# Attention output with probabilities as the stationary operand, V plus a column of ones as the moving one, scaled with tokens on partitions, transposed by DMA

## The chip, the cores and the metric

The kernel runs on one core of a Trainium2 chip. The metric is device time in microseconds (us) of one execution, of the slowest core; here there is only one. A kernel is run several times, and its time is the median. A profile comes from one execution, so its span can lie anywhere in the spread of the timed runs.

Engines in the profile are PE (TensorE matmuls), PEld (TensorE weight loads), DVE (VectorE), ACT (ScalarE), POOL (GpSimd) and SP (SyncE, which issues most DMAs here). A matmul has a stationary operand (`lhsT`, which a weight load puts into the array) and a moving operand (`rhs`, which streams through it). PSUM is the memory that matmuls write to, divided into banks; SBUF is the one from which they read. To evict a PSUM tile is to copy it out, so that its bank can be used again. A semaphore, a DMA or a bank that an instruction needs can make it wait; where the text says that A waits for B, the profile inferred it. "L1064" is line 1064 of the kernel whose profile is shown.

## The reference, cut to what matters

```python
def _A_ref(x, k_cache, v_cache, wq, wo):     # x: (1, 2048, 1024), 32 query heads, 4 kv heads, Dh = 128
    W = min(4096, max(256, Sk // 4))         # 512 keys per head
    q = (x @ wq) ...                         # heads apart
    k, v = last W rows of the caches, repeated 8 times
    scores = einsum('bhqd,bhkd->bhqk', q, k) * Dh ** (-0.5)
    p = softmax(scores)
    o = einsum('bhqk,bhkd->bhqd', p, v)
    return o (heads side by side) @ wo

mod = silu(c) @ w_mod                        # six vectors: sa, ca, ga, sb, cb, gb
h = layernorm(x) * (1 + ca) + sa
x = x + ga * _A_ref(h, ...)
h = layernorm(x) * (1 + cb) + sb
x = x + gb * ((silu(h @ w_gate) * (h @ w_up)) @ w_down)
```

All inputs are bfloat16. (`...` marks what is cut or told in words.)

## The kernel before

The attention part runs 128 steps: 4 chunks of 512 tokens times 32 heads. One step is, on PE: 4 matmuls of scores (`s_ps`), 8 of a later head's query projection (`q_ps`), 8 of an earlier group's output projection (`a_ps`), and 4 that multiply probabilities with V (`o_ps`). Each has 512 moving columns. Scores are kept with keys on partitions, so a softmax row sum is a sum over partitions. The kernel before makes it in three parts: VectorE adds the four key blocks (`psA`, `psB`), once in four steps four matmuls with a block of ones add over partitions (`l_ps`, each using 32 columns of the array), and the reciprocals travel through DRAM to be broadcast to all partitions (`rb`), where VectorE multiplies them into `oT`.

```python
# ... pools: blkC has 10 buffers of 4 KB per partition, PSUM tag "mm" has 4 banks
def emit_s(g):
    # ... s_ps matmuls; pT = exp(scale * s_ps) on ScalarE
    a = wk.tile([P, 2, TCW], BF16, name="psA", tag="psA", bufs=2)
    nc.vector.tensor_tensor(out=a, in0=p[:, 0:2, :], in1=p[:, 2:4, :], op=ALU.add)
    b = wk.tile([P, TCW], BF16, name="psB", tag="psB", bufs=5)
    nc.vector.tensor_tensor(out=b, in0=a[:, 0, :], in1=a[:, 1, :], op=ALU.add)
    rec[g] = b

def emit_l(g):                                   # every fourth step
    l_ps = mm("l_ps")
    for i in range(4):
        nc.tensor.matmul(l_ps[32 * i:32 * i + 32, :], lhsT=ones_bf[:, 0:32],
                         rhs=rec.pop(g - 3 + i), start=True, stop=True)
    r = wk.tile([P, TCW], FP32, name="rinv", tag="f32", bufs=2)
    nc.scalar.activation(out=r, in_=l_ps, func=ACT.Ln)
    nc.scalar.activation(out=r, in_=r, func=ACT.Exp, scale=-1.0)
    # ... DMA to DRAM; load_rb broadcasts it back; emit_norm: oT = oT * rb on VectorE

def emit_o(g):
    # ... a new oT tile every four heads
    o_ps = mm("o_ps")
    for j in range(WT):                          # 4 key blocks
        nc.tensor.matmul(o_ps, lhsT=v_sb[:, kv, j, :], rhs=pT[g][:, j, :],
                         start=(j == 0), stop=(j == WT - 1))
    nc.scalar.copy(out=oT[(cc, hg)][:, hi, :], in_=o_ps)

def emit_wo(cc, q, u):                           # 8 matmuls; q = 0 opens a sum:
    # ...
    nc.vector.tensor_copy(out=acc[(cc, t)][:, dsl], in_=a_ps)

def load_cols(n, k, dst, add_one):               # a modulation vector, turned to columns
    # ... fetch(out=dst, in_=src)                # a small DMA
    if add_one:
        nc.vector.tensor_scalar(out=dst, in0=dst, scalar1=1.0, scalar2=None, op0=ALU.add)

# the loop of steps
for k in range(NU + 1):
    # ... emit_s(k), emit_q(k + LEAD), then the tasks planned for step k (emit_wo among them)
    if k >= 1:
        if k % 4 == 0:
            emit_l(k - 1)
        emit_o(k - 1)
# ... then the feed-forward part: gu_ps (gate and up) and d_ps (down) matmuls
```

## Time and profile before

Three runs give a median of 1292.92 us (1292.06 to 1293.39).

| | before |
|---|---|
| span of the profiled execution | 1290.1 us |
| PE busy | 1271.4 us, 99% |
| VectorE / ScalarE busy | 653.1 us, 51% / 433.7 us, 34% |
| moved by DMA | 221.08 MB |
| start to start of 512-column matmuls | 0.216 us |
| four steps, start to start | 21.16 us |

The first fence is from the page of the profile of the kernel before: span, busy time by engine (microseconds, share of the span, instructions), and the chain of work that ended last (followed back from the last instruction, at each step to what released it), as shares of the span by engine and by line.

```profile
span 1290.1 us, 15319 instructions
...
PE 1271.4 (99%) x6073; PEld 577.4 (45%) x6193; DVE 653.1 (51%) x1159; ACT 433.7 (34%) x625; POOL 1.2 (0%) x7
...
PE 95%; SPq 2%; DMA 1%; DVE 1%; issue 1%; DVEq 0%
PE gu_ps L1168 29%; PE a_ps L1095 17%; PE q_ps L1018 17%; PE d_ps L1188 15%; PE o_ps L1079 9%; PE s_ps L1031 8%; SPq L664 1%; PE l_ps L1048 1%; SPq L703 1%; DMA hT<-xn 0%; DMA wq<-in_A_wq_dram 0%; DMA wu<-in_B_w_up_dram 0%; PE row_ps L777 0
```

PE is the engine that decides: 95% of the chain is PE. What VectorE and ScalarE do costs nothing as long as no matmul waits for it. Busy PE time is of little use for a closer reading, because the ends of matmuls are modelled and overlap small gaps. Starts are better.

The next view is the groups of instructions of the kernel before: line, engine, operation, output and inputs, shapes, count | busy us and mean ns of one | idle time of the engine before them and what ended most of it.

```profile
L1079 PE MATMUL o_ps<-pT,v_sb 128*128 128x512 bf16 x510 | 131.5, 380 | 0.2
...
L1038 DVE TENSOR_TENSOR psA<-pT 128x1024 bf16<-128x1024 bf16 x128 | 87.8, 686 | 89.0 <-ACT pT L1033 88.9
...
L1069 DVE TENSOR_TENSOR oT<-oT,rb 128x1024 bf16<-128x1024 bf16 x64 | 75.4, 1218 | 1.5 <-DMA rb<-r_d 1.5
L1081 ACT CAST oT<-o_ps 128x512 bf16<-128x512 f32 x128 | 74.5, 582 | 166.4 <-PE o_ps L1079 166.4
...
L1040 DVE TENSOR_TENSOR psB<-psA 128x512 bf16<-128x512 bf16 x128 | 53.4, 417 | 0.6
...
L1048 PE MATMUL l_ps<-psB,ones_bf 128*32 128x512 bf16 x128 | 12.8, 389 | 0.3
...
L1188 PE MATMUL d_ps<-wd,guT 128*128 128x128 bf16 x56 | 3.3, 219 | 0.0
```

The mean of 380 ns for a 512-column matmul is the time from its start to its modelled end, not the time PE needs for one: the next starts 216 ns later. The three VectorE groups are 217 us of work that the change takes away, and that PE never waits for. The `l_ps` group is 12.8 us busy, but what it costs has to be read from the timeline.

This is the timeline of PE in the kernel before, in one steady part: start in us, duration, engine, line, operation, count.

```profile
344.49 1.03 PE L1079 MATMUL o_ps<-pT,v_sb 128*128 128x512 bf16 x4
345.35 1.03 PE L1031 MATMUL s_ps<-qT,kT 128*128 128x512 bf16 x4
346.21 1.89 PE L1018 MATMUL q_ps<-hT,wq 128*128 128x512 bf16 x8
347.94 1.89 PE L1095 MATMUL a_ps<-wo,oT 128*128 128x512 bf16 x8
349.76 0.40 PE L1048 MATMUL l_ps<-psB,ones_bf 128*32 128x512 bf16 x4
350.09 1.04 PE L1079 MATMUL o_ps<-pT,v_sb 128*128 128x512 bf16 x4
350.97 1.03 PE L1031 MATMUL s_ps<-qT,kT 128*128 128x512 bf16 x4
```

Read differences of starts. A plain `o_ps` group is 344.49 to 345.35, 0.86 us for four matmuls, and a group of eight 1.73 us (346.21 to 347.94). The `a_ps` group that starts at 347.94 should thus be over at 349.67, but `l_ps` starts at 349.76 (0.09 lost); it lasts 0.33 until `o_ps` starts, and that `o_ps` takes 0.88 instead of 0.86. So one `l_ps` group costs 0.09 + 0.33 + 0.02 = 0.44 us. Starts of single matmuls say the same: 0.309 us from the last `a_ps` matmul to the first `l_ps` one, 3 ns between the four, 0.322 us to the first of `o_ps`. The four run beside each other in 32-column tiles. Of the 0.44 us, 0.22 is what one 512-column matmul takes anyway, and the other 0.22 is lost on entering and leaving.

For the new cost the trace of before holds one sample, the last `d_ps` matmuls of the program, which have 128 columns and a new weight load each. They start 55.8 ns apart. The last line of the view above agrees: 3.3 us, less the 0.219 of the last one, over 55 spacings is 56 ns. How VectorE evicts tiles of such widths shows in the timeline of VectorE at the end of the kernel before (in brackets: idle time before it, and what ended that).

```profile
1281.81 0.42 DVE L1192 TENSOR_TENSOR f_10710<-d_ps,gb_bc 128x256 f32<-128x256 f32 x1 [1.64 <-PE d_ps L1188]
...
1283.38 0.29 DVE L1192 TENSOR_TENSOR f_10744<-d_ps,gb_bc 128x128 f32<-128x128 f32 x1 [0.68 <-PE d_ps L1188]
```

An eviction of 256 columns took 0.42 us and one of 128 columns 0.29 us.

### The profile page before, as it was taken

The page shows a single profiled execution, that of the slowest core. Times are in us where ns is not written, and L with a number is a line of the kernel's source. Part 1 is how long each engine was busy: PE and PEld are TensorE (multiplying, and loading weights), DVE is VectorE, ACT ScalarE, POOL GpSimd, SP SyncE. Part 2 cuts the span into 40 slices and gives each one's busy share as a digit, 9 for nine tenths or more (in the row PEclk, how much of TensorE's full clock was granted, in tenths as well). Part 3 has the DMA queues.
Part 4 walks back from the last instruction along what each step waited for, and adds up shares of the span by engine and source line. Part 5 has one row for each costly group of instructions (what it writes and reads, how often), then busy time and mean ns, then how long its engine had stood idle before and what let it go on. Part 6 is the DMA issues. An engine that isn't in the chain of part 4 may idle for free.

```text
span 1290.1 us, 15319 instructions
## 1 busy us (share of the span) xinstructions
PE 1271.4 (99%) x6073; PEld 577.4 (45%) x6193; DVE 653.1 (51%) x1159; ACT 433.7 (34%) x625; POOL 1.2 (0%) x7
## 2 busy tenths in 40 slices
PE   8999999999999999999999999999999999999998
PEld 4444444444444444444444444444444444444444
DVE  5575668976688867597865641222122111222122
ACT  4755545554555555555552111011100111011100
POOL 0000000000000000000000000000000000000000
PEclk9999999999999999999999999999999999999999
DMA  9788565567365655455657485454536445454402
GB/s 290 242 277 256 178 196 139 170 174 219 103 193 144 189 146 175 146 165 143 185 194 238 127 240 182 136 192 131 171 105 220 157 148 178 135 192 131 147 18 84
DMA packets 219939, 221.08 MB, mean 171 GB/s; under 512 B 45385, under 2 KB 205129, under 8 KB 219858
## 3 DMA queue, kind: packets, MB, share of 16 engines
q1 hardware_dynamic: 214690, 215.54, 54.5%
q10 hardware_dynamic: 5168, 4.46, 1.0%
q8 instruction: 50, 0.82, 0.3%
q14 instruction: 31, 0.25, 0.1%
HBM read 207.63 MB, written 4.47 MB: 164 GB/s over the span
## 4 chain that ended last, share of the span: by engine, by line
PE 95%; SPq 2%; DMA 1%; DVE 1%; issue 1%; DVEq 0%
PE gu_ps L1168 29%; PE a_ps L1095 17%; PE q_ps L1018 17%; PE d_ps L1188 15%; PE o_ps L1079 9%; PE s_ps L1031 8%; SPq L664 1%; PE l_ps L1048 1%; SPq L703 1%; DMA hT<-xn 0%; DMA wq<-in_A_wq_dram 0%; DMA wu<-in_B_w_up_dram 0%; PE row_ps L777 0%; DVE guT L1174 0%; DVE xn L833 0%
## 5 line engine op out<-in xcount | busy, mean ns | idle before, releaser
L1033 ACT ACTIVATE pT<-s_ps 128x1024 bf16<-128x1024 f32 x256 | 252.0, 1026 | 72.8 <-PE s_ps L1031 67.3
L1095 PE MATMUL a_ps<-wo,oT 128*128 128x512 bf16 x972 | 238.9, 379 | 2.6
L1018 PE MATMUL q_ps<-hT,wq 128*128 128x512 bf16 x994 | 236.1, 379 | 0.8 <-DVE modT L753 0.3
L1173 ACT ACTIVATE sg<-gu_ps 128x512 bf16<-128x512 f32 x112 | 66.9, 597 | 486.0 <-PE gu_ps L1168 420.4
L1174 DVE TENSOR_TENSOR guT<-gu_ps,sg 128x512 bf16<-128x512 f32 x112 | 77.4, 691 | 280.0 <-ACT sg L1173 280.0
L1168 PE MATMUL gu_ps<-hT,wu 128*128 128x512 bf16 x878 | 210.1, 379 | 2.6 <-DMA wu<-in_B_w_up_dram 1.7
L1168 PE MATMUL gu_ps<-hT,wg 128*128 128x512 bf16 x877 | 210.0, 379 | 1.1
L1188 PE MATMUL d_ps<-wd,guT 128*128 128x512 bf16 (+2 forms) x934 | 193.2, 366 | 0.9
L1095 PEld LDWEIGHTS <-oT 128*128 128x128 bf16 x1024 | 100.0, 98 | 121.4 <-issue 1.3
L1018 PEld LDWEIGHTS <-wq 128*128 128x128 bf16 x1000 | 97.8, 98 | 118.5 <-DMA wq<-in_A_wq_dram 0.7
L1188 PEld LDWEIGHTS <-guT 128*128 128x128 bf16 x952 | 90.9, 98 | 103.0
L1168 PEld LDWEIGHTS <-wu 128*128 128x128 bf16 x896 | 87.6, 98 | 107.8 <-DMA wu<-in_B_w_up_dram 2.2
L1168 PEld LDWEIGHTS <-wg 128*128 128x128 bf16 x896 | 87.7, 98 | 105.7
L1038 DVE TENSOR_TENSOR psA<-pT 128x1024 bf16<-128x1024 bf16 x128 | 87.8, 686 | 89.0 <-ACT pT L1033 88.9
L1031 PE MATMUL s_ps<-qT,kT 128*128 128x512 bf16 x508 | 131.1, 379 | 0.7 <-ACT pT L1033 0.6
L1079 PE MATMUL o_ps<-pT,v_sb 128*128 128x512 bf16 x510 | 131.5, 380 | 0.2
L1081 ACT CAST oT<-o_ps 128x512 bf16<-128x512 f32 x128 | 74.5, 582 | 166.4 <-PE o_ps L1079 166.4
L914 DVE CAST qT<-q_ps 128x512 bf16<-128x512 f32 x128 | 87.5, 685 | 78.6 <-PE q_ps L1018 77.9
L1031 PEld LDWEIGHTS <-kT 128*128 128x128 bf16 x512 | 50.1, 98 | 61.5 <-issue 1.5
L1069 DVE TENSOR_TENSOR oT<-oT,rb 128x1024 bf16<-128x1024 bf16 x64 | 75.4, 1218 | 1.5 <-DMA rb<-r_d 1.5
L1079 PEld LDWEIGHTS <-v_sb 128*128 128x128 bf16 x512 | 47.4, 98 | 60.3 <-issue 7.7
L1040 DVE TENSOR_TENSOR psB<-psA 128x512 bf16<-128x512 bf16 x128 | 53.4, 417 | 0.6
(279 smaller groups left out, 443.2 us busy)
## 6 DMA issues: line engine op xcount, KB each, us to landing
wq<-in_A_wq_dram SPq DMA_DIRECT2D x64, 512.0 KB
rb<-r_d SPq DMA_DIRECT2D x64, 512.0 KB
wo<-in_A_wo_dram SPq DMA_DIRECT2D x64, 512.0 KB
wg<-in_B_w_gate_dram SPq DMA_DIRECT2D x56, 512.0 KB
wu<-in_B_w_up_dram SPq DMA_DIRECT2D x56, 512.0 KB
wd<-in_B_w_down_dram SPq DMA_DIRECT2D x56, 512.0 KB
wmr<-in_w_mod_dram SPq DMA_DIRECT2D x8, 1024.0 KB
out_dram<-o_sb ACTq DMA_DIRECT2D x31, 128.0 KB
```

The costliest lines, as they stand in the source:

```text
L914: nc.vector.tensor_copy(out=t, in_=q_ps)
L1018: nc.tensor.matmul(q_ps, lhsT=wq_tiles[(cc, h // 4, dt // 4)][:, dt % 4, (h % 4) * P:(h % 4 + 1) * P], rhs=hT[("h1", cc)][:, dt, :], start ...
L1031: nc.tensor.matmul(s_ps[:, i, :], lhsT=kT[:, kv, j * P:(j + 1) * P], rhs=qT[g], start=True, stop=True)
L1033: nc.scalar.activation(out=p[:, 2 * jj:2 * jj + 2, :], in_=s_ps, func=ACT.Exp, scale=scale)
L1038: nc.vector.tensor_tensor(out=a, in0=p[:, 0:2, :], in1=p[:, 2:4, :], op=ALU.add)
L1069: pin(nc.vector.tensor_tensor(out=oo, in0=oo, in1=rb, op=ALU.mult))
L1079: nc.tensor.matmul(o_ps, lhsT=v_sb[:, kv, j, :], rhs=pT[g][:, j, :], start=(j == 0), stop=(j == WT - 1))
L1081: nc.scalar.copy(out=oT[(cc, hg)][:, hi, :], in_=o_ps)
L1095: nc.tensor.matmul(a_ps, lhsT=oT[(cc, 2 * q + i)][:, hh % 4, t * P:(t + 1) * P], rhs=wo_tiles[(cc, q, dh, i)][:, hh % 4, :], start=(hh == ...
L1168: nc.tensor.matmul(ps[:, n, :], lhsT=gu_w[(cc, fg, nm, dt // 4)][:, dt % 4, fi * P:(fi + 1) * P], rhs=hT[("h2", cc)][:, dt, :], start=(dt ...
L1174: nc.vector.tensor_tensor(out=guT[(cc, fg)][:, fi, :], in0=ps[:, 1, :], in1=g, op=ALU.mult)
L1188: nc.tensor.matmul(d_ps, lhsT=guT[(cc, f // 4)][:, f % 4, t * P:(t + 1) * P], rhs=wd_tiles[(cc, dh, f // 4)][:, f % 4, c0:c0 + w], start=( ...
```

## The change

The intent is to get rid of the `l_ps` matmuls on PE and of the whole row-sum machinery. P becomes stationary, a 128x128 block of keys by tokens, and V moves, with a column of ones added: 129 columns, of which the last is the row sum. The result has tokens on partitions, so the reciprocal is one value per partition, and VectorE scales while it evicts. But then the result lies the wrong way round for the output projection, and DMAs have to transpose it, four transposes of 128x512 for each four heads. The 512 `o_ps` matmuls of 512 columns become 2048 of 129, each with its own weight load.

```diff
-    pc_ = ctx.enter_context(tc.tile_pool(name="blkC", bufs=10))
+    pc_ = ctx.enter_context(tc.tile_pool(name="blkC", bufs=13))
 ...
-    v_sb = blkB("v_sb", [P, Hkv, WT, Dh])
+    VW = Dh + 4
+    v_sb = blkB("v_sb", [P, Hkv, WT, VW])
     for kv in range(Hkv):
-        load(v_sb[:, kv], v_v[:, kv])
+        load(v_sb[:, kv, :, 0:Dh], v_v[:, kv])
+    nc.gpsimd.memset(v_sb[:, :, :, Dh:VW], 1.0)
 ...  psA, psB, emit_l, load_rb, emit_norm removed
+    SLOTS = 3
+    def close_bank():
+        ps, runs = o_slot["ps"], o_slot["runs"]
+        n = o_slot["n"]
+        rl = sm.tile([P, SLOTS], FP32, name="rl", tag="rl", bufs=4)
+        nc.vector.reciprocal(out=rl[:, 0:n], in_=ps[:, 0:n, Dh])
+        for g, t0, t1, s0 in runs:
+            cnt = t1 - t0
+            dst = oq[(g // H, (g % H) // 4)][:, t0:t1, g % 4, :]
+            sc = rl[:, s0:s0 + cnt].unsqueeze(2).to_broadcast([P, cnt, Dh])
+            nc.vector.tensor_tensor(out=dst, in0=ps[:, s0:s0 + cnt, 0:Dh], in1=sc, op=ALU.mult)
+        o_slot.update(n=0, runs=[])
 ...  emit_o
-        for j in range(WT):
-            nc.tensor.matmul(o_ps, lhsT=v_sb[:, kv, j, :], rhs=pT[g][:, j, :],
-                             start=(j == 0), stop=(j == WT - 1))
-        nc.scalar.copy(out=oT[(cc, hg)][:, hi, :], in_=o_ps)
+        for t in range(QT):
+            if o_slot["n"] == 0:
+                o_slot["ps"] = mm("o_ps", (P, SLOTS, Dh + 1))
+            s_ = o_slot["n"]
+            for j in range(WT):
+                nc.tensor.matmul(o_slot["ps"][:, s_, :], lhsT=pT[g][:, j, t * P:(t + 1) * P],
+                                 rhs=v_sb[:, kv, j, 0:Dh + 1], start=(j == 0),
+                                 stop=(j == WT - 1))
+            ...  after three slots: close_bank()
+    def xpose_o(cc, hg):
+        src = oq.pop((cc, hg))
+        dst = oT[(cc, hg)] = blkC("oT", [P, 4, TCW])
+        for t in range(QT):
+            pin(nc.sync.dma_start_transpose(
+                out=dst[:, :, t * P:(t + 1) * P],
+                in_=src[:, t, :, :].rearrange("p h d -> p (h d)")), "dma")
 ...
     for g in range(3, NU, 4):
-        at(g + 2, load_rb, g)
-        at(g + 4, emit_norm, g)
+        at(g + 3, xpose_o, g // H, (g % H) // 4)
```

Cut: scratch tiles that got another tag, and the bookkeeping of which head's columns lie in which slot.

More of the change, by code (lines that the diff above doesn't have):

```diff
@@ L950, in bound_wq @@
         w = wq_tiles[(1 + hg % (NTC - 1), hg, i)][:, 2 * j:2 * j + 2, :]
-        junk = wk.tile([P, 2, 512], BF16, name="junk", tag="psA", bufs=2)
+        junk = wk.tile([P, 2, 512], BF16, name="junk", tag="junk", bufs=1)
         col = (hg * 2 + i) * 2 + j
@@ L965, in bound_k @@
             i = kv * WT + j
-            junk = wk.tile([P, Dh], BF16, name="junk", tag="psA", bufs=2)
+            junk = wk.tile([P, Dh], BF16, name="junk", tag="junk", bufs=1)
             src = k_ld[0][:, kv, j, :]
@@ L1008, in fast_path @@
     oT = {}
-    rec = {}
-    rinv = {}
+    oq = {}
     acc = {}
@@ L1036, in emit_s @@
         pT[g] = p
-        a = wk.tile([P, 2, TCW], BF16, name="psA", tag="psA", bufs=2)
-        nc.vector.tensor_tensor(out=a, in0=p[:, 0:2, :], in1=p[:, 2:4, :], op=ALU.add)
-        b = wk.tile([P, TCW], BF16, name="psB", tag="psB", bufs=5)
-        nc.vector.tensor_tensor(out=b, in0=a[:, 0, :], in1=a[:, 1, :], op=ALU.add)
-        rec[g] = b
-    def emit_l(g):
-        l_ps = mm("l_ps")
-        for i in range(4):
-            nc.tensor.matmul(l_ps[32 * i:32 * i + 32, :], lhsT=ones_bf[:, 0:32],
-                             rhs=rec.pop(g - 3 + i), start=True, stop=True)
-        r = wk.tile([P, TCW], FP32, name="rinv", tag="f32", bufs=2)
-        nc.scalar.activation(out=r, in_=l_ps, func=ACT.Ln)
-        nc.scalar.activation(out=r, in_=r, func=ACT.Exp, scale=-1.0)
-        d = dp.tile([4, TCW], FP32, name="r_d", tag="r_d", bufs=4)
-        nc.scalar.dma_start(out=d, in_=r[0:P:32, :])
-        rinv[g // 4] = d
-    def load_rb(g):
-        d = rinv[g // 4]
-        rinv[g // 4] = []
-        for i in range(2):
-            rb = wk.tile([P, 2, TCW], FP32, name="rb", tag="rb", bufs=2)
-            fetch(out=rb, in_=d[2 * i:2 * i + 2, :].partition_broadcast(P))
-            rinv[g // 4].append(rb)
-    def emit_norm(g):
-        o = oT[(g // H, (g % H) // 4)]
-        for i, rb in enumerate(rinv.pop(g // 4)):
-            oo = o[:, 2 * i:2 * i + 2, :]
-            pin(nc.vector.tensor_tensor(out=oo, in0=oo, in1=rb, op=ALU.mult))
+    SLOTS = 3
+    o_slot = {"n": 0, "runs": []}
+    def close_bank():
[9 more added lines that the diff above has]
+        o_slot.update(n=0, runs=[])
     def emit_o(g):
@@ L1073, in emit_o @@
         kv = h // rep
-        hg, hi = h // 4, h % 4
-        if hi == 0:
-            oT[(cc, hg)] = blkC("oT", [P, 4, TCW])
-        o_ps = mm("o_ps")
-        for j in range(WT):
-            nc.tensor.matmul(o_ps, lhsT=v_sb[:, kv, j, :], rhs=pT[g][:, j, :],
-                             start=(j == 0), stop=(j == WT - 1))
-        nc.scalar.copy(out=oT[(cc, hg)][:, hi, :], in_=o_ps)
-        del pT[g]
+        if h % 4 == 0:
+            oq[(cc, h // 4)] = blkC("oq", [P, QT, 4, Dh])
+        for t in range(QT):
[6 more added lines that the diff above has]
+                                 stop=(j == WT - 1))
+            runs = o_slot["runs"]
+            if runs and runs[-1][0] == g:
+                runs[-1][2] = t + 1
+            else:
+                runs.append([g, t, t + 1, s_])
+            o_slot["n"] = s_ + 1
+            if o_slot["n"] == SLOTS or (t == QT - 1 and h % HQ == HQ - 1):
+                close_bank()
+        del pT[g]
+    def xpose_o(cc, hg):
[5 more added lines that the diff above has]
+                in_=src[:, t, :, :].rearrange("p h d -> p (h d)")), "dma")
     def load_wo(cc, q, dh, i):
@@ L1214, in fast_path @@
         if k >= 1:
-            if k % 4 == 0:
-                emit_l(k - 1)
             emit_o(k - 1)
```

## The prediction

> **What bounds the kernel now.** TensorE. The page's first part has PE busy 99% of 1290.1 us, and the chain of waits is 95% PE. The timeline shows PE packed: every 512-column matmul starts 0.216 us after the one before it, and between 50 and 750 us I find under 1 us of other gaps. VectorE (51%) and ScalarE (34%) never hold PE up, and DMA (54.5% of queue time) does so once, 1.9 us at about 762 us. So only PE's own time counts, plus any new wait.
>
> **Removed from PE.** 32 groups of four l_ps matmuls (row sums). The four start 3 ns apart, but there are 0.309 us from the last a_ps matmul to it instead of 0.216, then 0.322 us to the next o_ps. One group lengthens a step (5.18 us, else 5.61) by 0.42 us: 32 x 0.424 = 13.6 us.
>
> **Exchanged on PE.** 512 o_ps matmuls of 512 columns (4 per head, 0.864 us) become 2048 of 129 columns, each with its own 128x128 weight load. The Trainium skill, "TensorE: Matmul & The Clock Gate", section "Back-to-back issue gap", gives about 81 ns per matmul for a stream of load-matmul pairs at N=128; that would cost 128 x (1.30 - 0.864) = 55 us (estimate). This trace disagrees: the last d_ps matmuls, 128 columns wide with a new load each, start 55.8 ns apart, and the one-column mod_ps pairs 25 ns apart, so loads hide. I take the measurement: 129 columns, about 56.2 ns, 0.899 us per head, +4.5 us in all.
>
> **Off the critical path.** VectorE loses psA (87.8 us), psB (53.4) and the oT scaling (75.4), about 217 us; it gains 176 reciprocals (about 0.17 us each) and 256 scaled evictions from PSUM. By the d_ps evictions (0.69, 0.42, 0.29 us for 512, 256, 128 columns) these take 0.56, 0.42 or 0.29 us: together 108 + 30 = 138 us. VectorE falls to about 575 us. ScalarE loses the oT casts (74.5) and Ln/Exp of l (39.3): about 320 us. rb broadcasts (33.5 MB) go; 128 transposes of 128 KB (16.8 MB) come, each perhaps 0.7 us of SP issue (estimate from the hT transposes of twice the size, 1.26 us median). oT is read 15 us later at the earliest.
>
> **Possible new waits.** An o_ps bank stays open across heads, but q_ps and a_ps keep banks of their own and o_ps alternates between two, so a bank has about one step (5 us) from closing to reuse; the worst VectorE chain in a step is about 3.3 us. I allow 1 us in total.
>
> **Predicted.** 1292.9 - 13.6 + 4.5 + 0.7 = 1284.5 us, 0.65% faster. Range 1280 to 1292. Faster by over 2%: 0.02; within 2%: 0.93; slower by over 2%: 0.05.
>
> **Right or wrong in the profile.** o_ps: 2048 matmuls 56 ns apart, no gap before the next s_ps; step length constant at about 5.21 us instead of 5.18/5.61; l_ps gone; VectorE near 575 and ScalarE near 320 us busy; no PE idle before a_ps put down to the oT transposes, and none before o_ps or q_ps put down to oq.
>
> **What would make it wrong.** Weight loads not hidden over long runs (81 ns: +50 us); 129-column output at 516-byte slot offsets being slower per matmul (each ns is 2 us); o_ps banks freed late by VectorE, in steps with layer norm or the final wo sums; transposes behind loads in SP's one queue arriving after a_ps wants them.

## The result, and the profile after

The changed kernel's four runs give a median of 1287.34 us (1285.61 to 1289.6), beside 1293.16 (1292.06 to 1293.42) for four runs of the kernel before. The ratio is 0.9958, with a 95% interval of 0.9944 to 0.9972: 0.42% faster, inside the 2% that count as the same. A ratio is the mean time of one kernel's runs over the mean of the other's of the same rounds, so it is not quite the ratio of the medians that are quoted. Executions over 1.5% slower than the fastest of the same kernel are left out of the means. The runs of the changed kernel spread over 4 us, those of before over 1.4 us, and the profile of after is of its slowest run. A second measurement in other rounds (told below) gave 1286.07 beside 1292.74.

The page of the profile of the changed kernel:

```profile
span 1287.8 us, 18140 instructions
...
PE 1272.8 (99%) x7601; PEld 644.0 (50%) x7601; DVE 577.8 (45%) x1271; ACT 334.0 (26%) x433; POOL 1.3 (0%) x8
...
PE 95%; DMA 2%; DVE 1%; SPq 1%; ACT 0%; issue 0%; DVEq 0%
PE gu_ps L1168 29%; PE a_ps L1096 17%; PE q_ps L1019 17%; PE d_ps L1188 15%; PE o_ps L1064 9%; PE s_ps L1032 8%; DMA wm<-in_w_mod_dram 1%; SPq L664 1%; DMA modT<-row_d 0%; DMA hT<-xn 0%; DMA wu<-in_B_w_up_dram 0%; PE row_ps L779 0%; PE q_ps
```

The span shrinks by 2.3 us in these two profiled executions, and PE's busy time even grows from 1271.4 to 1272.8 us, although PE has less to do. This growth is not real. The profile of before lacks the records of 120 matmuls (PE x6073 beside PEld x6193; after, both are 7601), and 117 holes of 52 or 53 ns in it, 6.2 us in all, are where one is missing. VectorE fell by 75 us and ScalarE by 100 us, and none of that is on the chain. DMA moved 204.20 MB instead of 221.08.

The groups of the changed kernel that took the place of those above:

```profile
L1064 PE MATMUL o_ps<-v_sb,pT 128*128 128x129 bf16 x2048 | 139.2, 219 | 0.0
...
L1051 DVE TENSOR_TENSOR oq<-o_ps,rl 128x256 bf16<-128x256 f32 (+2 forms) x256 | 101.3, 420 | 4.3
...
L1046 DVE RECIPROCAL rl<-o_ps 128x3 f32<-128x3 f32 (+1 forms) x176 | 28.0, 164 | 0.0
```

The new VectorE work, 101.3 + 28.0 us, stands against the 217 us that left. The timeline of PE in the changed kernel, in a steady part:

```profile
343.75 1.09 PE L1064 MATMUL o_ps<-v_sb,pT 128*128 128x129 bf16 x16
344.68 1.02 PE L1032 MATMUL s_ps<-qT,kT 128*128 128x512 bf16 x4
...
348.99 1.09 PE L1064 MATMUL o_ps<-v_sb,pT 128*128 128x129 bf16 x16
349.92 1.03 PE L1032 MATMUL s_ps<-qT,kT 128*128 128x512 bf16 x4
```

All steps are now alike: `o_ps` takes 0.92 to 0.93 us (343.75 to 344.68; 348.99 to 349.92) where it took 0.86, and `s_ps` follows with no gap. From 344.68 to 349.92 one step is 5.24 us. From the starts of all steps: four steps take 20.955 us, where the kernel before took 21.16.

The sum over the 128 steps can be checked against one stretch of both profiles. From the first `s_ps` matmul to the first `gu_ps` matmul the kernel before needs 655.50 us and the changed one 649.80, which is 5.7 us less and nearly the whole difference of the medians, 5.8. The remaining 3.5 us by which the two profiled spans disagree lie outside that stretch: the first `s_ps` starts 1.4 us later, at 27.66 instead of 26.30, and the feed-forward part is 2.1 us longer. Neither need be of the change as such. One kernel profiled twice (the last experiment below, the same kernel as in "272-byte rows, and the addition of 1 later") started its first `s_ps` at 25.91 and at 28.09. And the feed-forward part shows a wait, in the timeline of PE of the changed kernel:

```profile
755.16 1.03 PE L1168 MATMUL gu_ps<-hT,wu 128*128 128x512 bf16 x4
758.26 1.04 PE L1168 MATMUL gu_ps<-hT,wu 128*128 128x512 bf16 x4 [2.08 <-DMA wu<-in_B_w_up_dram]
759.14 3.16 PE L1168 MATMUL gu_ps<-hT,wg 128*128 128x512 bf16 x8
```

Between the two `gu_ps` groups PE waited for a weight load. This wait is in the kernel before too (1.91 us of it, at 762 us). But the next eight matmuls take 3.16 us where they otherwise take 1.89: their starts are 0.427 us apart instead of 0.216, for 3.41 us, in which the profile's record of the granted clock is 0.50 (759.6 to 763.0 us); this loses about 1.7 us. In the profile of before the matmuls after the wait keep 0.216. The Trainium skill, "TensorE: Matmul & The Clock Gate", Part 1 ("The HAM clock gate"), says that the matmul clock is halved after idle windows of about 3.4 us, free-running. The trace agrees with the length of the slow stretch (3.41 us), but the gap here was only 2.24 us beyond the usual 0.216, and not every such gap did it: see the last point of the last section.

Two more lines of the changed kernel are needed for the one new wait. First VectorE, around 90 us:

```profile
88.04 0.54 DVE L835 TENSOR_SCALAR xn<-x,mv 128x1024 bf16<-128x1024 bf16 x1
92.22 0.17 DVE L802 TENSOR_SCALAR modT<-modT 128x8 f32<-128x8 f32 x1 [3.63 <-DMA modT<-row_d]
92.30 0.69 DVE L816 BATCH_NORM_STATS2 st<-x 128x6 f32<-128x512 bf16 x1
92.90 0.67 DVE L1102 COPY acc<-a_ps 128x512 f32<-128x512 f32 x1
```

Then PE in the same stretch:

```profile
90.75 1.89 PE L1019 MATMUL q_ps<-hT,wq 128*128 128x512 bf16 x8
93.62 1.24 PE L1096 MATMUL a_ps<-wo,oT 128*128 128x512 bf16 x5 [0.99 <-DVE acc L1102]
```

At 88.6 us it came to the addition of 1 to a modulation vector (`modT`), whose small DMA had not yet landed, and waited 3.63 us. Behind it in VectorE's order stood the eviction `acc<-a_ps`, and PE needed that bank back: it waited for `acc`, and four steps there took 23.19 us instead of the 22.24 of before. With the 0.2 us that any four steps gained, 22.04 was to be expected, so this wait costs 1.15 us. In the kernel before, the same addition ran at the same time, and VectorE's timeline shows what stood there:

```profile
88.51 2.35 DVE L1069 TENSOR_TENSOR oT<-oT,rb 128x1024 bf16<-128x1024 bf16 x2
...
91.24 0.68 DVE L1101 COPY acc<-a_ps 128x512 f32<-128x512 f32 x1
92.23 0.17 DVE L800 TENSOR_SCALAR modT<-modT 128x8 f32<-128x8 f32 x1 [0.31 <-DMA modT<-row_d]
```

VectorE was busy with the scaling of `oT` (two of them, 2.35 us) while the DMA was under way, the eviction went ahead of the addition, and only 0.31 us of waiting was left. The change took that scaling away, and VectorE came to the addition earlier. But the two kernels also differ in order: before, the eviction stands ahead of the addition, after the change behind it. The change did not touch the lines of either, and why the build put them in another order is not shown. With the old order the eviction would not have stood behind the DMA.

Last, from the DMA issues of the changed kernel: output and input, queue, operation, count, and median us from issue to landing.

```profile
oT<-oq SPq DMA_TRANSPOSE x128, 2.4
...
hT<-xn SPq DMA_TRANSPOSE x28, 2.8
```

The transposes of `oT` land after 2.4 us. In the timeline of SP each takes 1.25 us to issue (the median), and the four of a group take 5.1 us where nothing else holds them, and up to 7.8. They land 9 to 18 us before `a_ps` first reads them, mostly 13 to 16, and PE never waited for one.

### The profile page after: what moved, and what is told of

The parts are those of the page before. It is cut to its first block, busy times and chain, and to the rows that moved or that the text cites. A ratio compares the mean times of both kernels' runs of the same rounds, so it can differ in the third digit from the quotient of the medians.

```text
span 1287.8 us, 18140 instructions
## 1 busy us (share of the span) xinstructions
PE 1272.8 (99%) x7601; PEld 644.0 (50%) x7601; DVE 577.8 (45%) x1271; ACT 334.0 (26%) x433; POOL 1.3 (0%) x8
## 2 busy tenths in 40 slices
DMA packets 280107, 204.20 MB, mean 159 GB/s; under 512 B 113865, under 2 KB 273609, under 8 KB 280018
## 4 chain that ended last, share of the span: by engine, by line
PE 95%; DMA 2%; DVE 1%; SPq 1%; ACT 0%; issue 0%; DVEq 0%
PE gu_ps L1168 29%; PE a_ps L1096 17%; PE q_ps L1019 17%; PE d_ps L1188 15%; PE o_ps L1064 9%; PE s_ps L1032 8%; DMA wm<-in_w_mod_dram 1%; SPq L664 1%; DMA modT<-row_d 0%; DMA hT<-xn 0%; DMA wu<-in_B_w_up_dram 0%; PE row_ps L779 0%; PE q_ps L940 0%; DVE st L816 0%; SPq L848 0%; ACT pT L1034 0%
## 5 line engine op out<-in xcount | busy, mean ns | idle before, releaser
L1034 ACT ACTIVATE pT<-s_ps 128x1024 bf16<-128x1024 f32 x256 | 248.6, 1020 | 345.4 <-PE s_ps L1032 345.4
L1096 PE MATMUL a_ps<-wo,oT 128*128 128x512 bf16 x1024 | 241.9, 379 | 1.0 <-DVE acc L1102 1.0
L1168 PE MATMUL gu_ps<-hT,wg 128*128 128x512 bf16 x896 | 212.9, 381 | 0.0
L1064 PEld LDWEIGHTS <-pT 128*128 128x128 bf16 x2048 | 128.4, 97 | 30.6 <-issue 0.4
L1064 PE MATMUL o_ps<-v_sb,pT 128*128 128x129 bf16 x2048 | 139.2, 219 | 0.0
L1051 DVE TENSOR_TENSOR oq<-o_ps,rl 128x256 bf16<-128x256 f32 (+2 forms) x256 | 101.3, 420 | 4.3
L1192 DVE TENSOR_TENSOR f<-d_ps,gb_bc 128x512 f32<-128x512 f32 (+2 forms) x34 | 22.4, 660 | 147.1 <-PE d_ps L1188 147.1
L1104 DVE TENSOR_TENSOR acc<-a_ps,acc 128x512 f32<-128x512 f32 x64 | 44.1, 688 | 40.8 <-PE a_ps L1096 40.8
L1032 PEld LDWEIGHTS <-kT 128*128 128x128 bf16 x512 | 44.7, 97 | 31.9 <-issue 1.3
L816 DVE BATCH_NORM_STATS2 st<-x 128x6 f32<-128x512 bf16 x64 | 41.3, 680 | 2.7 <-DMA x<-in_A_x_dram 2.5
```

The source lines that it names most:

```text
L1032: nc.tensor.matmul(s_ps[:, i, :], lhsT=kT[:, kv, j * P:(j + 1) * P], rhs=qT[g], start=True, stop=True)
L1034: nc.scalar.activation(out=p[:, 2 * jj:2 * jj + 2, :], in_=s_ps, func=ACT.Exp, scale=scale)
L1051: nc.vector.tensor_tensor(out=dst, in0=ps[:, s0:s0 + cnt, 0:Dh], in1=sc, op=ALU.mult)
L1064: nc.tensor.matmul(o_slot["ps"][:, s_, :], lhsT=pT[g][:, j, t * P:(t + 1) * P], rhs=v_sb[:, kv, j, 0:Dh + 1], start=(j == 0), stop=(j == W ...
L1096: nc.tensor.matmul(a_ps, lhsT=oT[(cc, 2 * q + i)][:, hh % 4, t * P:(t + 1) * P], rhs=wo_tiles[(cc, q, dh, i)][:, hh % 4, :], start=(hh == ...
L1104: nc.vector.tensor_tensor(out=acc[(cc, t)][:, dsl], in0=a_ps, in1=acc[(cc, t)][:, dsl], op=ALU.add)
```

## Experiments

The theory after the first reading is a sum of three terms: PE gains 32 groups of `l_ps` at 0.44 us (14.1 us), loses 128 times 0.059 us by the slower `o_ps` (7.5 us), and loses about 1 us to the wait at 94 us. The rivals were that the `l_ps` gain is smaller and hidden elsewhere, that `o_ps` is slow for another reason than it seems (odd column count, slot offset in PSUM, the row start of V in SBUF, weight loads), and that the transposes cost time in the queue.

The spacings in `o_ps` pointed at one of those: they are not even, but alternate 56 and 59.5 ns. The slow ones are the odd key blocks, whose V rows start at an odd multiple of 8 bytes (a row is 132 elements, 264 bytes).

### V rows of 272 bytes

```diff
-    VW = Dh + 4
+    VW = Dh + 8
```

> One change to the changed kernel: the V rows are 136 elements apart (272 bytes) and not 132 (264 bytes). In the changed kernel's trace the o_ps matmuls start 56 and 59.5 ns apart in turn, the slow ones being those whose V row starts at an odd multiple of 8 bytes. Theory A (the slow half is the start of the moving row off a 16-byte boundary): all 2048 start about 56 ns apart, the o_ps group of a head takes 0.896 us and not 0.923, a step 5.21 and not 5.24 us, and the kernel is about 1024 x 3.5 ns = 3.6 us faster than the changed kernel (about 1283.5 us). Rival B (an odd number of columns, or the odd matmul of a pair as such, is slow): the two spacings stay and the time does not move.

Measured: 1285.85 us (1284.95 to 1286.92, five runs) beside 1293.47 of before (11 runs), ratio 0.994 (0.9927 to 0.9953). The alternation is gone: all spacings are 56.7 ns, and four steps take 20.89 us instead of 20.955. PE's timeline of this kernel:

```profile
348.77 1.07 PE L1064 MATMUL o_ps<-v_sb,pT 128*128 128x129 bf16 x16
349.68 1.03 PE L1032 MATMUL s_ps<-qT,kT 128*128 128x512 bf16 x4
```

The `o_ps` group is 0.91 us (348.77 to 349.68) where the changed kernel has 0.92 to 0.93. By the steps this is worth 0.065 us in four, 2.1 us in 128. The expectation was larger, since the even blocks, 55.9 ns before, rose to 56.7. That the pitch of the V rows, and so where they start, makes the alternation is shown; why the even ones rose is not. The Trainium skill, "SBUF — State Buffer", section "Specifications (TRN2)", says that SBUF has lines of 16 bytes and that crossing to a new line is penalised. That alone does not explain the alternation: by this line size a row of 258 bytes touches 17 lines whether it starts on a line or 8 bytes into one (an estimate, if `v_sb` starts on a line). What the runs show is the size: 57.7 ns on average with rows of 264 bytes, 56.7 with 272. In time it is within the spread of runs here (see the repeats below).

### 130 columns instead of 129

```diff
-                o_slot["ps"] = mm("o_ps", (P, SLOTS, Dh + 1))
+                o_slot["ps"] = mm("o_ps", (P, SLOTS, Dh + 2))
 ...
-                                 rhs=v_sb[:, kv, j, 0:Dh + 1], start=(j == 0),
+                                 rhs=v_sb[:, kv, j, 0:Dh + 2], start=(j == 0),
```

> One change to the changed kernel: 130 moving columns (two of ones) and 130 PSUM columns a slot, rows still 264 bytes apart. Theory A (row start off 16 bytes): spacings of about 56.5 and 60 ns stay in turn. Rival B (an odd column count): all equal, about 56.7 ns. It also puts every PSUM slot on an 8-byte boundary (520 bytes and not 516), so if the slot offset were the cause, slots 1 and 2 would get faster here.

Measured: one run, 1287.6 us, span 1285.7. The spacings alternate between 55.9 and 59.5 ns, as in the changed kernel. So neither the odd number of columns is the reason nor the 516-byte offset of the slots, which the prediction had named as a risk.

### The kernel before without its l_ps matmuls

```diff
-        l_ps = mm("l_ps")
-        for i in range(4):
-            nc.tensor.matmul(l_ps[32 * i:32 * i + 32, :], lhsT=ones_bf[:, 0:32],
-                             rhs=rec.pop(g - 3 + i), start=True, stop=True)
 ...
-        nc.scalar.activation(out=r, in_=l_ps, func=ACT.Ln)
+        nc.scalar.activation(out=r, in_=rec.pop(g), func=ACT.Ln)
```

This computes wrong row sums (they are not added over partitions); VectorE, ScalarE and the DMAs do all that they did before. The comparison with the reference does not see this error, and says little about the scaling of the attention.

> The kernel before without its 128 l_ps matmuls (the logarithm reads one head's psB in place of l_ps, so the output is wrong on purpose); everything else, VectorE, ScalarE and DMA work of the row sums too, stays. Theory (one half of the change is the 32 stand-alone groups on TensorE): 32 x 0.43 us = 13.7 us faster than the kernel before, about 1279.5 us, all steps 5.18 us long. Rival (the gain of the change comes from the lighter VectorE, ScalarE and DMA): within 2 us of the kernel before.

Measured: 1278.93 us (1278.45 to 1279.47, four runs), ratio 0.9889 (0.9874 to 0.9903), 14.5 us less than the 1293.47 of before. PE's timeline:

```profile
346.57 1.89 PE L1091 MATMUL a_ps<-wo,oT 128*128 128x512 bf16 x8
348.29 1.03 PE L1075 MATMUL o_ps<-pT,v_sb 128*128 128x512 bf16 x4
```

`o_ps` follows `a_ps` after 1.72 us, as any group of eight does, and all steps take 5.18 us. Four steps are 20.72 us against 21.16. So the `l_ps` groups cost 0.44 us each, 14.1 us in all, which the time confirms with 14.5, and the rival falls: this gain came with none of the VectorE, ScalarE and DMA work taken away. This kernel is also the measure of what the change gave back: it is what the change would have been worth if `o_ps` had stayed as it was.

### The changed kernel with the l_ps matmuls put back

```diff
+    def emit_l(g):
+        l_ps = mm("l_ps")
+        for i in range(4):
+            nc.tensor.matmul(l_ps[32 * i:32 * i + 32, :], lhsT=ones_bf[:, 0:32],
+                             rhs=pT[g][:, i, :], start=True, stop=True)
+        l_sb = sm.tile([P, 4], FP32, name="l_sb", tag="l_sb", bufs=2)
+        nc.scalar.copy(out=l_sb, in_=l_ps[:, 0:4])
 ...
+            if k % 4 == 0:
+                emit_l(k - 1)
```

> The changed kernel with 32 groups of four 32-column l_ps matmuls put back at the same places (they read probabilities, and only 4 columns are copied out; the result is right). Theory (the group's cost is TensorE's own time): 13 to 15 us slower than the changed kernel, about 1301 us, every fourth step 0.43 us longer. Rival (the groups cost only through what reads them): within 2 us of the changed kernel.

Measured: 1300.9 us (1299.15 to 1301.88, six runs), ratio 1.0056 (1.0044 to 1.0068), 13.6 us more than the changed kernel's 1287.34 in other rounds. PE's timeline:

```profile
354.00 1.89 PE L1104 MATMUL a_ps<-wo,oT 128*128 128x512 bf16 x8
355.82 0.40 PE L1080 MATMUL l_ps<-pT,ones_bf 128*32 128x512 bf16 x4
356.15 1.09 PE L1064 MATMUL o_ps<-v_sb,pT 128*128 128x129 bf16 x16
```

`a_ps` to `l_ps` is 1.82 us where a group of eight has 1.73, then 0.33 to `o_ps`: the same 0.44 us as in the kernel before, in another neighbourhood, and four steps take 21.39 us instead of 20.955. The Trainium skill, "TensorEngine Tiling (Array Packing)", section "Key Properties", says that changing the tiling mode drains TensorE. It has no figure. The runs fit this, though they do not show that a drain is the reason, and give a figure: four tiled matmuls that start within 10 ns of each other cost 0.44 us, if they stand alone among untiled ones.

### 272-byte rows, and the addition of 1 later

```diff
-            nc.vector.tensor_scalar(out=dst, in0=dst, scalar1=1.0, scalar2=None, op0=ALU.add)
+            at(16 * n + 20, plus_one, dst)
+
+    def plus_one(dst):
+        pin(nc.vector.tensor_scalar(out=dst, in0=dst, scalar1=1.0, scalar2=None, op0=ALU.add))
```

(on top of the 272-byte rows)

> The run with 272-byte V rows, and the one-time addition of 1 to a modulation vector (VectorE, waiting for a small DMA) moved four steps later. In the changed kernel's trace TensorE waits 1.15 us once, at 93.6 us, for the eviction of a_ps, and VectorE had waited 3.63 us for that small DMA just before. Theory (VectorE in order stands behind the DMA and holds back the eviction of the one bank that a_ps has): that wait goes, and the time falls by 1.0 to 1.4 us against the run with 272-byte rows, to about 1284.7 us. Rival (VectorE is late there from its own work, layer norm statistics and the scaled evictions): the wait stays within 0.3 us.

Measured: 1284.59 us (1282.68 to 1285.21, five runs) beside 1292.81 of before, ratio 0.9937 (0.9923 to 0.9951). PE's timeline where the wait was:

```profile
88.76 1.89 PE L1022 MATMUL q_ps<-hT,wq 128*128 128x512 bf16 x8
90.48 1.89 PE L1099 MATMUL a_ps<-wo,oT 128*128 128x512 bf16 x7
```

`a_ps` follows `q_ps` after 1.72 us, with no wait; four steps there take 21.98 us, which in the kernel with 272-byte rows alone were 23.36. So the wait was VectorE's order, as read: counted from the first `s_ps`, the DMA lands no earlier (after 64.2 us, and 64.5 with 272-byte rows alone), only the instruction that needs it is later. The trace shows 1.4 us gained. The medians of the two kernels, taken in different rounds, differ by 1.26 us, but their ratios to before, 0.994 and 0.9937, do not resolve it.

### A fourth buffer for the layer norm rows

```diff
-    pc_ = ctx.enter_context(tc.tile_pool(name="blkC", bufs=13))
+    pc_ = ctx.enter_context(tc.tile_pool(name="blkC", bufs=12))
 ...
-        n = wk.tile([P, D], BF16, name="xn", tag="xn", bufs=3)
+        n = wk.tile([P, D], BF16, name="xn", tag="xn", bufs=4)
```

(on top of the previous one). The theory was that the late weight load at 758 us came late because SP, in order, stood before a transpose of layer norm rows that waited for a buffer.

> The run before this one, plus a fourth buffer for the normalised rows (paid for with one blkC buffer of 13). Both kernels' traces show TensorE idle once in the feed-forward, near 758 us (1.9 us before, 2.1 us after), for a wu load whose issue stood behind a transpose whose input waited for a free buffer; in the changed kernel's trace 3.4 us at half clock follow it (1.7 us more). Theory: the idle time goes, and with it the chance of half clock; 1.8 us faster than the run before this one, up to 3.5 where that one shows the half clock; about 1282.5 us. Rival (the wu load is late from DMA bandwidth): the idle time stays. If 13 blkC buffers were needed, new PE waits for oT or wo would show.

Measured: 1283.88 us (1283.37 to 1285.33, five runs), ratio 0.9935 (0.9921 to 0.9948), not told apart from the previous one. PE's timeline:

```profile
751.20 1.03 PE L1171 MATMUL gu_ps<-hT,wu 128*128 128x512 bf16 x4
753.70 1.04 PE L1171 MATMUL gu_ps<-hT,wu 128*128 128x512 bf16 x4 [1.47 <-DMA wu<-in_B_w_up_dram]
```

The wait is still there, 1.47 us beside 1.72 in the previous kernel. The last transpose no longer waits for a buffer of the rows, but the four together still take 6.33 us to issue. The weight load follows them by 0.09 us, at 749.51 us, and lands 4.14 us later; the profile puts its release down to PE, which frees its buffer at about that time. Which of the two held it is not settled, but the buffer of the rows was not what made the wait. What would take this wait away was not tried further, since it is in the kernel before as well.

### Every oT transpose issued twice

```diff
+        twice = wk.tile([P, 4, TCW], BF16, name="twice", tag="twice", bufs=1)
 ...  after each transpose into dst, the same one again:
+            pin(nc.sync.dma_start_transpose(
+                out=twice[:, :, t * P:(t + 1) * P],
+                in_=src[:, t, :, :].rearrange("p h d -> p (h d)")), "dma")
```

(on the changed kernel, with blkC at 12 to make room; nothing reads the second copy)

> The changed kernel with every oT transpose issued twice, the second into a buffer that nobody reads (12 blkC buffers and not 13 for room). In the changed kernel a group's four transposes take 5.1 to 5.3 us of the queue's issue and land about 13 us before their first use. Theory (transposes are off the critical path with slack): 128 x 1.25 us = 160 us more issue time, PE step length unchanged at 5.24 us, time within 1.5 us of the changed kernel. Rival (transposes near the edge): waits of PE for oT or for weights, over 5 us more.

Measured: 1308.81 us (1307.04 to 1309.94, four runs), ratio 1.012 (1.0105 to 1.0136), 21 us more than the changed kernel's 1287.34. The steady steps are unchanged at 20.955 us in four. The waits of the profile that grew (who waits, for whom: us in total, times, longest):

```profile
DVE modT L802 <- DMA modT<-row_d: 8.7, 1, 8.7
...
PE gu_ps L1172 <- DMA wu<-in_B_w_up_dram: 7.2, 2, 5.4
...
PE q_ps L1019 <- DMA wq<-in_A_wq_dram: 5.8, 1, 5.8
...
PE q_ps L1019 <- DVE qT L916: 5.3, 1, 5.3
```

Nothing waits for `oT`, but the expected "within 1.5 us" was wrong and the rival, waits for other loads, held. Three times PE stands for 5.3 to 5.8 us: for a `wq` load, for `qT` behind VectorE's wait of 8.7 us for that same small `modT` DMA, and for a `wu` load. All of these are issued by SP, one after the other, in stretches where its timeline is full. Each stall brings one stretch of 6.8 us at the half clock, of which 3.3 to 5.8 us lie after PE has gone on; that loses about 7 us more (estimate: half of the 13.5 us). So the second transposes cost in three places alone. That it is the time they take in SP's queue is shown for `wq`, where the chain of waits runs through eight transposes (62 to 75.6 us); for the other two it is argued, as the second copies also load the DMA engines (that `wu` load took 7.9 us to land, where the median in the changed kernel is 5.6). For the real ones it says that they cost nothing in the steady part, and where more of them would hurt. It does not say that the single transposes cost nothing at all in those three places.

### 128 columns: the price of the column of ones

```diff
-                                 rhs=v_sb[:, kv, j, 0:Dh + 1], start=(j == 0),
+                                 rhs=v_sb[:, kv, j, 0:Dh], start=(j == 0),
 ...
-        nc.vector.reciprocal(out=rl[:, 0:n], in_=ps[:, 0:n, Dh])
+        nc.vector.reciprocal(out=rl[:, 0:n], in_=ps[:, 0:n, 0])
```

(on top of the 272-byte rows; wrong, as a V column stands in for the row sums: relative error 0.025).

> The run with 272-byte V rows, with 128 moving columns, so without the column of ones (the reciprocal reads another column; wrong on purpose). By the 128-column d_ps matmuls of the trace: 55.8 ns apart. If the 129th column costs what its share of the width says, 272-byte rows at 129 columns should have shown 56.2 ns; they showed 56.7. So here 55.8 ns means 0.9 ns for the one column, 1.9 us in all; 56.3 or more would mean that something other than the column (the stationary operand, the slot offset) costs the rest.

Measured: one run, 1285.85 us, span 1284.1. Spacings average 56.1 ns (55 to 58) and four steps take 20.86 us instead of 20.89. That lies between the two values for which the expectation had a reading. The extra column itself is 0.5 to 0.6 ns per matmul, about 1 us in all (0.03 us in four steps), and with 128 columns the stream still stands 0.3 ns above the 55.8 of the `d_ps` sample. The 0.059 us per step by which `o_ps` is slower than in the kernel before thus divide, by steps: 0.016 for the row start of V, 0.008 for the column of ones, and 0.035 that four matmuls of 128 columns take longer than one of 512 (by the weight loads or by a fixed part of each matmul; the runs do not separate these).

### The changed kernel and the 272-byte rows again, in the same rounds

The changed kernel's first four times fell into 1285.6 to 1285.7 and 1289.0 to 1289.6, as if it had two modes. It was run again unchanged, with the 272-byte rows beside it.

> The changed kernel once more, in the same rounds as the two after it, so that the small differences are compared on one chip: 1286 to 1289 us. Theory (a one-time 3.4 us at half clock after the idle time at 758 us, seen in one profile, is what splits its earlier times into 1285.6 and 1289.3): two clusters about 1.7 to 3.5 us apart again. Rival (the spread is chip-to-chip or start-up): one cluster.

Measured: 1286.07 us (1284.42 to 1288.23, five runs) beside 1292.74 (nine), ratio 0.995 (0.9936 to 0.9963). The five times lie in one spread; two modes are not supported. The spread has parts that the profiles show: the first `s_ps` starts anywhere between 25.9 and 28.2 us, and the waits that occur once, at 94 and at 758 us, vary by a microsecond or so.

> The run with 272-byte V rows once more, beside the changed kernel: by its steps (20.89 us for four against 20.955) 32 x 0.065 = 2.1 us faster than the changed kernel, if only the row pitch acts; within 0.5 us if the step difference is given back elsewhere.

Measured: 1286.17 us (1285.5 to 1286.44, five runs), ratio 0.9949 (0.9936 to 0.9963): no difference in time to the changed kernel, where about 2 us were expected. The steps again take 20.89 us in four. But its one-time waits were longer in its profile (0.44 us at 32 us; 1.38 against 0.92 at 94; 2.06 against 1.47 at 757), which took back about 1.5 us, and its attention stretch was 648.44 us against 649.57. So the steady gain is shown in the traces, and its worth in time is not resolved.

### The best version again

This is the kernel with 272-byte rows and the later addition, unchanged, in the same rounds as the two above.

> The 272-byte rows and the late addition once more, beside the changed kernel: 2.1 us for the rows and 1.1 to 1.4 us for the one-time wait, so 3.3 us faster than the changed kernel and about 9 us (0.7%) faster than the kernel before, near 1284 us.

Measured: 1285.33 us (1283.1 to 1286.45, five runs) beside 1292.74, ratio 0.994 (0.9927 to 0.9954). It is clearly faster than the kernel before, by 7.4 us. Against the changed kernel of the same rounds it is 0.7 us lower in the median, with overlapping intervals. That it beats the changed kernel is not shown by its time; only its attention stretch says so, 646.61 us against 649.57 in single profiles.

## Why the prediction was right

The prediction was 1284.5 us in a range of 1280 to 1292, and 1287.34 came out (1286.07 in the repeat). Its reasoning held for the two large terms, of which the second had the wrong size; the third, the new wait, was right by luck. The first term's number was right though a bracket of the prediction has two lengths interchanged: a step is 5.18 us without the group and 5.61 with it.

| step of the prediction | predicted | measured | by what |
|---|---|---|---|
| only PE's own time counts | 95% PE | 95% PE after, too; the `l_ps` gain comes also with all work of VectorE and ScalarE kept | page before and after; `l_ps` taken out of before |
| `l_ps` groups gone | -13.6 us | -14.1 us by steps; -14.5 and +13.6 in time when taken out of before and put back into after | two experiments |
| weight loads hide | 56.2 ns | 57.7 ns mean (56 and 59.5) | starts in the trace |
| `o_ps` in narrow matmuls | +4.5 us | +7.5 us (0.059 x 128) | steps of after against before without `l_ps` |
| new waits | +1 us, allowance | +1.15 us, once, at 94 us, not where it was allowed for | timeline |
| VectorE busy | about 575 us | 577.8 us | page |
| ScalarE busy | about 320 us | 334.0 us | page |
| SP issue of one transpose | 0.7 us | 1.25 us | timeline |
| PE waits for the transposes | none | none | waits |
| sum | -8.4 (it wrote the last two terms as +4.5 and +0.7) | -5.8 and -6.7 in two measurements; -14.1 + 7.5 + 1.15 = -5.5 by parts | |

The step that was mis-sized is "129 columns, about 56.2 ns, 0.899 us per head, +4.5 us in all". It measured 0.923 to 0.925 us per head and 7.5 us. The estimate came from one short sample (128 columns, rows aligned) and scaled the width. What it could not hold is the row start of V at odd multiples of 8 bytes: with 272-byte rows the mean fell by 1.0 ns per matmul, to 56.7, which is 2.1 us by the steps. Without it the term would have been about 5.4 us (7.5 less 2.1). The prediction listed a slower 129-column output at 516-byte slot offsets as a danger: right in kind (each ns is 2 us) and wrong in place, as the run with 130 columns showed.

The allowance of 1 us for new waits agrees with the 1.15 us by luck. The prediction had it for `o_ps` banks that VectorE frees late, and took `a_ps` to be safe in a bank of its own. No matmul waited for an `o_ps` bank; the one that waited was `a_ps`, behind a small DMA of which the prediction says nothing.

The important choice was to trust the trace over a stated figure. The Trainium skill, "TensorE: Matmul & The Clock Gate", section "Back-to-back issue gap", gives about 81 ns per matmul for load-matmul pairs at N=128 (128 moving columns), which would have put this term at 55 us (estimate of the prediction) and made the change a loss. This trace had 55.8 ns for such a stream, and after the change 2048 matmuls confirmed 57.7.

The transposes were issued at 1.25 us each, not at the 0.7 that was scaled down by size from transposes of twice the size. It did not matter, since SP had the time, but it is nearly twice what the prediction allowed, and the run with doubled transposes showed, for one of its stalls, that the queue is where such an error would become time. The 14 us of ScalarE above the estimate is overlap. Busy time is the union of instructions that overlap in the profile: the groups of ScalarE add up to 455 us before and 338 after, where the unions are 433.7 and 334.0. So 17 us of what was taken away had lain over other work, and `pT` fell by 3.4 us.

Two things stay open. One is what makes PE wait for a weight load at 758 us, and how to take that away: one theory fell. The other is how the start-up's two microseconds of spread come about.

## What to carry to other kernels

When one engine is 95% of the chain, cost a change in starts on that engine: 217 us less of VectorE work was worth nothing that the runs show, and 32 small groups of tiled matmuls were worth 14 us, half of it for entering and leaving. Narrow matmuls with a new weight load each need not be slow, but take a sample of that width from the trace, and try rows of the moving operand that start on multiples of 16 bytes (worth 1.0 ns of 57.7 here). In an engine's in-order queue, put an instruction that waits for a late DMA behind those that free PSUM, not ahead of them, and check that order again after a change; and count a transpose's issue time by the piece and not by its bytes.

## What the Trainium skill lacked or had wrong

- "TensorE: Matmul & The Clock Gate", section "Back-to-back issue gap": about 81 ns per matmul for a sustained stream of loads and matmuls at N=128 is too slow for this case; the same section's figure for a single matmul without its load, about 56 ns, fits it. The runs show 55.8 ns (128 columns, end of before), 56.7 ns (129 columns, rows of 272 bytes) and 57.7 ns (129 columns, rows of 264 bytes), over 2048 matmuls.
- "SBUF — State Buffer", section "Specifications (TRN2)": it states a penalty for crossing 16-byte lines without a size for matmuls, and nothing of what the start of a moving operand costs. With every second row 8 bytes off, 129 columns took 59.5 and 55.9 ns in turn, 57.7 on average; with all rows at multiples of 16 bytes, 56.7.
- "TensorEngine Tiling (Array Packing)", section "Key Properties": it says that a change of tiling mode drains TensorE, and not how long. Here 0.309 us in and 0.322 us out, where 0.216 is usual, and 0.44 us for the whole of a lone group of four.
- "Advanced Engine Details and Errata", section "X-Bar Transpose (TRN2)": it calls transposes as fast as other DMAs. It leaves out the issue: 1.25 us of SP for 128 KB, 1.24 to 1.26 us for 256 KB, where a plain 512 KB weight load takes 0.37 to 0.53 us (medians). I found no page with the issue time of a transpose of these shapes on this chip.
- "TensorE: Matmul & The Clock Gate", Part 1: it ties the half clock to idle windows of about 3.4 us. Here gaps at about 758 us of 2.46 and 2.43 us, from start to start, were followed by 3.41 us of half clock in two profiles (the changed kernel, and the one with 128 columns), and one of 2.41 us (the best version again) and the shorter ones of the others were not; about 1.7 us are lost each time. No length of gap that decides it can be read from so few. The three gaps of 5.7 to 6.2 us in the run with doubled transposes each brought 6.83 us of half clock.
